# Weight loads held by a copied column, more conversion in the first order, inversion pieces behind softplus, and L in a spare tile

## The chip, the cores and the metric

The kernel runs on one core of one Trainium2 chip. The metric is device time in microseconds (us) of one launch; what is reported for a kernel is the median of several runs. The engines are PE (TensorE, matmuls; PEld is its weight load), DVE (VectorE), ACT (ScalarE), POOL (GpSimd) and SP, whose queue issues the DMA transfers.

## The reference

Two parts follow one another. The first is a delta-rule recurrence over 768 tokens for 4 × 8 heads of width 48; the second is a small MLP with a softplus over the 3072 tokens. The MLP's weights come as 64-bit floats, all other inputs as float32.

```python
def _attn_ref(q, k, v, beta):
    k_n = k / (np.linalg.norm(k, axis=-1, keepdims=True) + 1e-06)
    for t in range(S):
        y[:, :, t] = np.einsum('bhd,bhde->bhe', q[:, :, t], state)
        v_old = np.einsum('bhde,bhd->bhe', state, kt)
        state = state + bt[:, :, :, None] * np.einsum('bhd,bhe->bhde', kt, vt - v_old)

def _moe_ref(x, w_in, w_out):
    h = x @ w_in
    g = np.maximum(h, 0.0) + np.log1p(np.exp(-np.abs(h)))
    return (g @ w_out).astype(np.float32)
```

## The kernel before, in words

**Attention.** The 768 tokens are 12 steps `s` of 64 tokens for all 32 heads. Within a step the recurrence needs the inverse of a triangular matrix per head, built from products of the keys (`gram`, L120 to L149). Two steps (a pair `u`) share one inversion on DVE (`invert`, L186 to L227): a transpose L199, masks L203 and L205, a copy L216 and then a substitution in many small pieces, each a product L220 and a sum L226. `finish` (L229) transposes the result into the tile `tt` (L232, L233). For the first pair only, u = 0 and u = 1 below N16 = 2, the inversion runs in blocks of 16 and `join` (L236) puts the blocks together with two products on PE (L243, L250), using a block L (`LDS`, L211 to L214) that was saved before. Then `cross_a` (L255), `arrange` (L268), `cross_b` (L276), `k_state`, `p_half` with `mask_p`, `u_all` (L312), `y_all` (L332) and `state` (L321) are products on PE, each with a copy on ACT or DVE that the next product waits for. So a step is a chain of short handoffs. The steps 0 and 1 use the blocks of u = 0, the steps 2 and 3 those of u = 1, and so on.

**MLP.** The output of a step, `x`, is a chunk of 256 tokens. For each chunk eight groups of two blocks `f` run: the first product (L462, into `ph`), softplus (ACT L466 to L468, then DVE L470, L472, L473, or L476 alone in the first chunk), and the second product (L445, into `po`), one group later. The first chunk uses float32 weights; later ones use weights split into two parts of a faster type (`split`, L410: ACT L413 and L415, DVE L416), and 18 matmuls for the first product where the first chunk has 6 per group.

**Weights.** The 16 weight tiles come as 64-bit floats and are converted to float32 on the chip (`weights`, L370): for each f ACT takes a magnitude (L381), DVE does four steps (L393, L396, L400, L403) and ACT copies the result (L406). At the start of the conversion of f the load of tile f + 4 is issued (L390 to L392), after a `memset` of one of its columns. It is a generator: each `next` gives one step of four, and `fill(n)` in the first part asks for n steps.

**What sets the order.** The first part, up to the line `fill(5)`, stands under a manual schedule for PE, DVE, ACT and POOL: these engines run it in the order in which it is written. SP and all that follows are ordered by a scheduler that estimates times, within the order of dependences. The main loop interleaves the MLP groups with attention steps; `invert_some(2)` after a group asks for two inversion pieces, and `attend` for as many attention steps as are due. Each engine runs its own list strictly in order, so an instruction that waits holds those behind it. Tiles with the same name share buffers: "gh" and "gl" have two buffers each and hold softplus' result; x0, x1, x2, x4 and w0 to w15 have one.

Of the kernel before, what the change touches and what calls it, by code (L numbers as in the profile page):

```python
# [35 lines left out]
def deltanet_moe(ctx, tc, kT, qT, kN, kI, vN, beta, wts, out):  # L36
# [149 lines left out]
    def invert(u, cT, ncT):  # L186

        n = QB if u < N16 else HB  # L190
        blocks = range(0, HB, n)
        lq = one.tile([P, HB, HB], F32, name="ltq")
        for a in blocks:
            nc.gpsimd.affine_select(
                out=Z[:, a:a + n, a:a + n],
                in_=ncT[:, a:a + n].unsqueeze(1).to_broadcast([P, n, n]),
                compare_op=ALU.is_gt, fill=0.0, base=0, pattern=[[1, n], [-1, n]],
                channel_multiplier=0)
        nc.vector.transpose(lq.rearrange("p j i -> p i j"), LTD[u].rearrange("p q i -> p i q"))  # L199
        yield  # L200
        for a in blocks:
            d = (slice(None), slice(a, a + n), slice(a, a + n))
            nc.vector.tensor_tensor(lq[d], lq[d], Z[d], op=ALU.mult)  # L203
            yield
            nc.vector.tensor_tensor(Z[d], lq[d],  # L205
                                    cT[:, a:a + n].unsqueeze(2).to_broadcast([P, n, n]),
                                    op=ALU.mult)
            yield
        if u < N16:
            for j in range(2):  # L210
                ld = LDS[2 * u + j] = two.tile([P, NP, HB], F32, name="gh")  # L211
                nc.gpsimd.memset(ld[:, :, QB:], 0.0)
                nc.scalar.activation(ld[:, :, 0:QB], LTD[u][:, j * NP:(j + 1) * NP, 0:QB],  # L213
                                     AF.Copy, scale=half)  # L214
        tmp = one.tile([P, HB, HB], F32, name="x0" if u == 0 else "work")
        nc.vector.tensor_copy(Z.rearrange("p a b -> p (a b)")[:, 0:HB * HB:HB + 1], cT)  # L216
        for j in range(n - 2, 0, -1):
            r = n - 1 - j
            for a in blocks:
                nc.vector.tensor_tensor(  # L220
                    tmp[:, a:a + r, 0:j],
                    Z[:, a + j + 1:a + n, a + j:a + j + 1].to_broadcast([P, r, j]),
                    lq[:, a + j:a + j + 1, a:a + j].to_broadcast([P, r, j]), op=ALU.mult)
            for a in blocks:
                z = Z[:, a + j + 1:a + n, a:a + j]
                nc.vector.tensor_tensor(z, z, tmp[:, a:a + r, 0:j], op=ALU.add)  # L226
            yield  # L227
# [8 lines left out]
    def join(s):  # L236

        tt = TT[s // 2][:, s % 2 * NP:(s % 2 + 1) * NP, :]
        w1 = two.tile([P, NP, QB], F32, name="gl")
        pw = ps_a.tile([P, NP, QB], F32, name="pa")  # L240
        for p in range(NP):
            for r in lo + hi:
                nc.tensor.matmul(pw[r, p, :], LDS[s][r, p, :], tt[r, p, QB:HB],  # L243
                                 start=True, stop=True)
        nc.scalar.copy(w1, pw)
        yield
        pz = ps_a.tile([P, NP, QB], F32, name="pa")
        for p in range(NP):
            for r in lo + hi:
                nc.tensor.matmul(pz[r, p, :], tt[r, p, HB:], w1[r, p, :], start=True, stop=True)  # L250
        nc.vector.tensor_tensor(tt[:, :, QB:HB], tt[:, :, QB:HB], pz, op=ALU.subtract)
        nc.vector.transpose(tt[:, :, HB:], tt[:, :, 0:HB])
        yield

    def cross_a(s):  # L255

        tt = TT[s // 2][:, s % 2 * NP:(s % 2 + 1) * NP, :]
        pm = ps_a.tile([P, NP, HB], F32, name="pa")
        for i, e, p, ab, t in quads:
            nc.tensor.matmul(pm[lo[t], p, :], OFF[s][hi[t], p, :], tt[hi[t], p, 0:HB],  # L260
                             start=True, stop=True)
        nc.scalar.activation(OFF[s][lo[0]], pm[lo[0]], AF.Copy, scale=-1.0)
        if s < 2:
            nc.vector.tensor_scalar(OFF[s][lo[1]], pm[lo[1]], -1.0, None, op0=ALU.mult)
        else:
            nc.scalar.activation(OFF[s][lo[1]], pm[lo[1]], AF.Copy, scale=-1.0)
# [9 lines left out]
    def cross_b(s):  # L276

        tt = TT[s // 2][:, s % 2 * NP:(s % 2 + 1) * NP, :]
        pm = ps_a.tile([P, NP, HB], F32, name="pa")
        for i, e, p, ab, t in quads:  # L280
            nc.tensor.matmul(pm[lo[t], p, :], tt[lo[t], p, HB:], OFF[s][lo[t], p, :],  # L281
                             start=True, stop=True)
        for h in range(2):
            copies[s < 2 and h](tt[lo[h], :, HB:], pm[lo[h]])


    def k_state(s):
# [24 lines left out]
    def u_all(s):  # L312
        pus = [ps_a.tile([P, NP // 2, D], F32, name="pa") for e in range(2)]
        for i, e, p, ab, t in quads:
            nc.tensor.matmul(pus[e][tk[ab], i, :], TT[s // 2][tk[t], s % 2 * NP + p, :],  # L315
                             NV[s][tk[t], p, :], start=True, stop=True)
        for e in range(2):
            for ab in range(2):
                copies[s < 2 and ab](be[tk[ab], ab, e, :, C:], pus[e][tk[ab]])  # L319

    def state(s):  # L321
        for g in range(2):
            pd = ps_a.tile([P, 8, D], F32, name="pa")
            for i in range(8):
                for ab in range(2):
                    at = (ab * NP + 8 * g + i) * QW
                    nc.tensor.matmul(pd[dr[ab], i, :], ki[:, ab, 8 * g + i, :],  # L327
                                     big[:, at + C:at + QW], start=True, stop=True)
            for ab in range(2):
                copies[s < 1 and ab](bv[dr[ab], ab, 8 * g:8 * g + 8, C:], pd[dr[ab]])  # L330

    def y_all(s):  # L332

# [36 lines left out]
    def weights():  # L370
# [15 lines left out]
        for f in range(NF):  # L386
            hw, lw = words(f)
            if f + AHEAD < NF:

                ST[f + AHEAD] = one.tile([P, 4 * DM], I32, name=f"w{f + AHEAD}")  # L390
                nc.vector.memset(ST[f + AHEAD][:, 0:1], 0)
                load_weights(f + AHEAD)  # L392
            nc.vector.tensor_scalar(ex.bitcast(F32), ex.bitcast(F32), 2.0 ** -15, 122880.0,  # L393
                                    op0=ALU.max, op1=ALU.min)
            yield
            nc.vector.tensor_scalar(ex, ex, 3, 0x3FFFFFF8, op0=ALU.logical_shift_left,  # L396
                                    op1=ALU.bitwise_and)
            after = magnitude(f + 1) if f + 1 < NF else None
            yield
            nc.vector.scalar_tensor_tensor(ex, hw, -2 ** 30, ex, op0=ALU.bitwise_and,  # L400
                                           op1=ALU.bitwise_or)
            yield
            nc.vector.scalar_tensor_tensor(ex, lw, 29, ex, op0=ALU.logical_shift_right,  # L403
                                           op1=ALU.bitwise_or)
            HF[f] = one.tile([P, 2 * DM], F32, name=f"w{f}")
            nc.scalar.copy(HF[f], ex.bitcast(F32))  # L406
            done[0], ex = f + 1, after
            yield
# [10 lines left out]
    def moe():  # L419
# [4 lines left out]
        for s in range(NS):  # L424
# [26 lines left out]
            for f0 in range(0, NF, 2):  # L451
# [17 lines left out]
                if s:  # L469
                    nc.vector.scalar_tensor_tensor(a, ph, 0.0, a, op0=ALU.max, op1=ALU.add)  # L470
                    g = [two.tile([P, 2, n], F32R, name=name) for name in ("gh", "gl")]
                    nc.vector.tensor_copy(g[0], a)  # L472
                    nc.vector.tensor_tensor(g[1], a, g[0], op=ALU.subtract)  # L473
                else:
                    g = [two.tile([P, 2, n], F32, name="gh")]
                    nc.vector.scalar_tensor_tensor(g[0], ph, 0.0, a, op0=ALU.max, op1=ALU.add)  # L476
                yield
                if late is not None:
                    late()
# [14 lines left out]
    def fill(n):  # L494
        for _ in range(n):
            next(conversion, None)
# [59 lines left out]
            yield  # L556
            background.append(invert(u, *cols[u]))

    background = []

    def invert_some(n):
        for _ in range(n):
            if background and next(background[0], 0) == 0:
                background.pop()

    kas = [one.tile([P, 2, NP, D], F32, name=name) for name in ("tt", "x2")]
    kas = [[t[:, j] for j in range(2)] for t in kas]
    with tc.manual_schedule(engines={ET.PE, ET.DVE, ET.Activation, ET.Pool}):
# [59 lines left out]
        next(jn)  # L628
        for g in range(2):
            mask_p(g, pts[g])  # L630
        run(jn)
        scale_v(0)
        cross_a(0)
        arrange(0)
        fill(2)
        cross_b(0)
        fill(2)
        u_all(0)
        next(nm)
        fill(2)  # L640
        y_all(0)
        jn = join(1)
        next(jn)
        fill(2)
        state(0)
        load_ki(1)
        run(jn)
        cross_a(1)
        arrange(1)
        for _ in range(3):  # L650
            next(nm)
        fill(3)
# [1 line left out]
        cross_b(1)  # L654
        load_v(2)
        cols[1] = run(nm)
        fill(5)

    def attention():
        nonlocal steps_done  # L660
# [110 lines left out]
```

## Time and profile before

| what | value |
|---|---|
| three runs | 718.11, 718.76, 719.0 us (median 718.76) |
| the profiled execution | 716.53 us, span 714.8 us, mean granted TensorE clock 0.956 |
| busy in that span | PE 631.6 us (88%), DVE 457.5 (64%), ACT 369.4 (52%), POOL 30.1 (4%) |
| bytes over DMA | 44.80 MB in 35095 packets |
| weight loads | 16 tiles of 768 KB |

The trace is of one execution. In a row of the timeline or of the chain the first number is the start in us from the span's start, the second the duration in us; "x18" is a number of instructions merged into the row, and in brackets stands how long the engine had been idle before it and what ended that. "issue" is a wait for nothing that the profile shows. Rows of the waits read: engine, tile and line that waited, what it waited for, the sum in us, how often, the longest. In a row of windows, after the stretch and its length, come busy time and instruction count of PE, PEld, DVE, ACT and POOL, then the clock, the DMA share and GB/s.

### The profile page before, as it was taken

To read this page: it belongs to the slowest core of one execution; us is meant where nothing else is said; L and a number is where in the kernel's file an instruction comes from. 1 tells how busy PE (TensorE), PEld (TensorE's weight loads), DVE (VectorE), ACT (ScalarE), POOL (GpSimd) and SP (SyncE) were. 2 spreads that over 40 slices of the span, in tenths; PEclk is the share of its full clock that TensorE was granted. 3 is DMA by queue.
4 is the path that set the end of the run, shared out by engine and by line. 5 is a ranking of instruction groups with operands and counts; after the bars stand their busy time and mean duration, and the time that the engine had idled before them with its cause. 6 is when DMAs were issued, how large, how long until landed. Compare 5 with 4: busy or idle time off the path is not lost.

```text
span 714.8 us, 24068 instructions
## 1 busy us (share of the span) xinstructions
PE 631.6 (88%) x10736; PEld 583.5 (82%) x10736; DVE 457.5 (64%) x976; ACT 369.4 (52%) x681; POOL 30.1 (4%) x56
## 2 busy tenths in 40 slices
PE   4448877858998899998899997999998999999997
PEld 3447655537898898997899997899997999999997
DVE  5834799866746993466993467984449964454443
ACT  3222377819844356464357465365663556544443
POOL 3100100000000000000001000001000000000000
PEclk9999899979797999998999999899999999999999
DMA  9974250000022021032031130120310300201000
GB/s 224 367 280 120 68 137 10 0 2 25 4 71 78 23 68 46 13 88 61 23 86 38 48 100 27 45 57 25 73 31 24 79 2 25 59 3 33 1 23 22
DMA packets 35095, 44.80 MB, mean 63 GB/s; under 512 B 21776, under 2 KB 27184, under 8 KB 34992
## 3 DMA queue, kind: packets, MB, share of 16 engines
q1 hardware_dynamic: 34992, 43.27, 21.2%
q8 instruction: 84, 1.38, 0.8%
q14 instruction: 19, 0.16, 0.1%
HBM read 36.27 MB, written 4.72 MB: 57 GB/s over the span
## 4 chain that ended last, share of the span: by engine, by line
PE 65%; DVE 21%; issue 6%; ACT 6%; DMA 2%; SPq 0%; POOL 0%; DVEq 0%; ACTq 0%; POOLq 0%
PE po L445 24%; PE ph L462 23%; DVE work L220 3%; PE pa L342 3%; DVE Z L226 3%; PE pa L301 2%; PE pa L260 2%; PE pa L327 2%; PE pa L281 2%; DVE ltq L199 1%; DVE a L470 1%; DVE big L308 1%; DVE ex L403 1%; PE pa L315 1%; PE pa L131 1%
## 5 line engine op out<-in xcount | busy, mean ns | idle before, releaser
L462 PE MATMUL ph<-x,w 128*128 128x256 f32 x1680 | 247.4, 299 | 16.6 <-DVE a L470 9.0
L462 PEld LDWEIGHTS ph<-x,w 128*128 128x128 f32 x1680 | 228.3, 197 | 26.0 <-DVE a L470 9.7
L445 PE MATMUL po<-w,gh 128*128 128x384 f32 x768 | 214.9, 367 | 8.1 <-DVE gh L472 4.2
L466 ACT ACTIVATE a<-ph 128x512 f32<-128x512 f32 x96 | 57.4, 598 | 214.3 <-PE ph L462 203.4
L470 DVE SCALAR_TENSOR_TENSOR a<-ph,a 128x512 f32<-128x512 f32 x88 | 60.6, 689 | 155.5 <-ACT a L468 155.1
L445 PEld LDWEIGHTS po<-w,gh 128*128 128x128 f32 x768 | 139.3, 195 | 20.3 <-issue 6.6
L445 PE MATMUL po<-w,gl 128*128 128x384 f32 x352 | 121.2, 344 | 0.2 <-DVE gl L473 0.2
L445 PEld LDWEIGHTS po<-w,gl 128*128 128x128 f32 x352 | 67.8, 193 | 1.1 <-DVE gl L473 0.7
L473 DVE TENSOR_TENSOR gl<-a,gh 128x512 fp32r<-128x512 f32 x88 | 60.7, 690 | 3.8 <-PE po L445 0.7
L467 ACT ACTIVATE a<-a 128x512 f32<-128x512 f32 x96 | 60.7, 633 | 2.8
L468 ACT ACTIVATE a<-a 128x512 f32<-128x512 f32 x96 | 60.7, 632 | 2.4
L220 DVE TENSOR_TENSOR work<-Z,ltq 128x84 f32<-128x84 f32 (+14 forms) x148 | 44.0, 304 | 3.3 <-ACT gh L213 0.6
L226 DVE TENSOR_TENSOR Z<-Z,work 128x84 f32<-128x84 f32 (+14 forms) x148 | 44.1, 305 | 2.9
L472 DVE CAST gh<-a 128x512 fp32r<-128x512 f32 x88 | 38.0, 432 | 7.8 <-PE po L445 4.4
L342 PEld LDWEIGHTS pa<-big 128*64 128x64 f32 x768 | 26.0, 145 | 7.6 <-ACT big L319 2.6
L342 PE MATMUL pa<-big 128*64 128x64 f32 x768 | 28.8, 232 | 3.4 <-ACT big L319 2.1
L308 DVE TENSOR_TENSOR big<-pa,maskP 64x512 f32<-64x512 f32 x44 | 30.2, 686 | 1.6 <-PE pa L301 1.0
L301 PE MATMUL pa<-big,kt 48*64 48x64 f32 x704 | 27.7, 231 | 1.6 <-ACT off L118 0.9
L274 POOL MEMSET tt<- 32x512 f32 x24 | 13.2, 550 | 368.1 <-PE pa L260 203.2
L319 ACT COPY big<-pa 64x384 f32<-64x384 f32 x44 | 20.6, 472 | 13.1 <-PE pa L315 12.5
L301 PEld LDWEIGHTS pa<-big,kt 48*64 48x64 f32 x704 | 25.1, 145 | 2.0 <-ACT off L118 1.1
L330 ACT COPY big<-pa 48x384 f32<-48x384 f32 x42 | 19.9, 474 | 8.9 <-PE pa L327 8.3
(104 smaller groups left out, 648.4 us busy)
## 6 DMA issues: line engine op xcount, KB each, us to landing
w<-wts SPq DMA_DIRECT2D x16, 768.0 KB, 11.7
kt<-kT SPq DMA_DIRECT2D x24, 192.0 KB, 4.2
big<-qT SPq DMA_DIRECT2D x24, 192.0 KB, 4.1
nv<-vN SPq DMA_DIRECT2D x12, 384.0 KB, 4.1
ki<-kI SPq DMA_DIRECT2D x24, 192.0 KB, 3.5
out<-ex SPq DMA_DIRECT2D x24, 192.0 KB, 1.9
ka<-kN SPq DMA_DIRECT2D x8, 384.0 KB, 3.2
x<-x SPq DMA_DIRECT2D x66, 32.0 KB, 2.1
```

The source lines that it names most:

```text
L220: nc.vector.tensor_tensor(tmp[:, a:a + r, 0:j], Z[:, a + j + 1:a + n, a + j:a + j + 1].to_broadcast([P, r, j]), lq[:, a + j:a + j + 1, a:a ...
L226: nc.vector.tensor_tensor(z, z, tmp[:, a:a + r, 0:j], op=ALU.add)
L301: nc.tensor.matmul(pt[tk[ab], i, :], kts[s % 3][dr[ab], 8 * g + i, :], bv[dr[ab], ab, 8 * g + i, 0:C], start=True, stop=True)
L342: nc.tensor.matmul(py[tk[ab], i, :], big[:, at + C:at + 2 * C], big[:, at:at + C], start=True, stop=True)
L445: nc.tensor.matmul(po[:, h, 0:DM], g[b][:, f - f0, h * P:(h + 1) * P], weight(f, a, DM, DM), start=(f == 0 and i == 0), stop=end)
L462: nc.tensor.matmul(ph[:, f - f0], weight(f, a, k * P, P), xr[b][k], start=(c == 0), stop=(c == len(terms1) * NK - 1))
L466: nc.scalar.activation(a, ph, AF.Abs)
L467: nc.scalar.activation(a, a, AF.Exp, scale=-1.0)
L468: nc.scalar.activation(a, a, AF.Ln, bias=1.0)
L470: nc.vector.scalar_tensor_tensor(a, ph, 0.0, a, op0=ALU.max, op1=ALU.add)
L472: nc.vector.tensor_copy(g[0], a)
L473: nc.vector.tensor_tensor(g[1], a, g[0], op=ALU.subtract)
```

## The change

Four edits are made together.

1. L, the lower block for the join, no longer takes a "gh" buffer of softplus; it lies in a tile of the name x1 (u = 0) or x2 (u = 1), which is free at that time. The join's intermediate `w1`, before in a "gl" buffer, lies in the same tile.
2. The column of the weight tile f + 4 that was set by a `memset`, which depends on nothing, is now copied from `ex`, the magnitude of conversion f. So the load of tile f + 4 waits for that magnitude.
3. For step 1 the second copies of `cross_a`, `cross_b` and `u_all`, which were on DVE, go to ACT; those of `state(0)` as well.
4. In the first part the calls of `fill` ask for 25 steps of conversion instead of 16, and some stand earlier; in the loop the inversion pieces are issued after the last softplus instruction that was written down before them.

```diff
         if u < N16:
+            spare = one.tile([P, 2, NP, HB + QB], F32, name=f"x{u + 1}")
             for j in range(2):
-                ld = LDS[2 * u + j] = two.tile([P, NP, HB], F32, name="gh")
+                ld = LDS[2 * u + j] = spare[:, j, :, 0:HB]
+                LDS[2 * u + j, 1] = spare[:, j, :, HB:]
...
-        w1 = two.tile([P, NP, QB], F32, name="gl")
+        w1 = LDS[s, 1]
...
-        if s < 2:
+        if s < 1:
             nc.vector.tensor_scalar(OFF[s][lo[1]], pm[lo[1]], -1.0, None, op0=ALU.mult)
...
-            copies[s < 2 and h](tt[lo[h], :, HB:], pm[lo[h]])
+            copies[s < 1 and h](tt[lo[h], :, HB:], pm[lo[h]])
...
-                copies[s < 2 and ab](be[tk[ab], ab, e, :, C:], pus[e][tk[ab]])
+                copies[s < 1 and ab](be[tk[ab], ab, e, :, C:], pus[e][tk[ab]])
...
-                copies[s < 1 and ab](bv[dr[ab], ab, 8 * g:8 * g + 8, C:], pd[dr[ab]])
+                nc.scalar.copy(bv[dr[ab], ab, 8 * g:8 * g + 8, C:], pd[dr[ab]])
...
-                nc.vector.memset(ST[f + AHEAD][:, 0:1], 0)
+                nc.vector.tensor_copy(ST[f + AHEAD][:, 0:1], ex[:, 0:1])
...
-                    nc.vector.tensor_tensor(g[1], a, g[0], op=ALU.subtract)
+                    softplus[0] = nc.vector.tensor_tensor(g[1], a, g[0], op=ALU.subtract)
...
     def invert_some(n):
-        for _ in range(n):
-            if background and next(background[0], 0) == 0:
-                background.pop()
+        with tc.issue_after(softplus[0].ins):
+            for _ in range(n):
+                if background and next(background[0], 0) == 0:
+                    background.pop()
...
+        fill(2)
         run(jn)
         scale_v(0)
+        fill(2)
         cross_a(0)
         arrange(0)
         fill(2)
         cross_b(0)
-        fill(2)
+        fill(3)
         u_all(0)
         next(nm)
-        fill(2)
+        fill(4)
         y_all(0)
         jn = join(1)
         next(jn)
-        fill(2)
+        fill(4)
         state(0)
...
         arrange(1)
+        fill(2)
...
-        fill(5)
+        fill(3)
```

The lines of the changed kernel are three higher from L211 on (L243 becomes L246, L260 becomes L263, L445 becomes L448, and so on), up to the softplus of the later chunks; numbers behind a tile's name are those of its buffers.

First, the queue of SP in the first part, behind the load of w3. Before, it holds the tiles w8 to w15 next:

```order
L368 DMA w3_114<-wts 128x1536
L368 DMA w8_1413<-wts 128x1536
L368 DMA w9_1424<-wts 128x1536
L368 DMA w10_1525<-wts 128x1536
L368 DMA w11_1536<-wts 128x1536
L368 DMA w12_1564<-wts 128x1536
L368 DMA w13_1575<-wts 128x1536
L368 DMA w14_1610<-wts 128x1536
L368 DMA w15_1621<-wts 128x1536
L95 DMA ka_1844<-kN 128x768
L79 DMA kt0_74<-kT 48x1024 x2
L368 DMA w4_740<-wts 128x1536
```

After the change, in the same place:

```order
L371 DMA w3_114<-wts 128x1536
L95 DMA ka_1840<-kN 128x768
L79 DMA kt0_74<-kT 48x1024 x2
L371 DMA w4_631<-wts 128x1536
L371 DMA w5_749<-wts 128x1536
L371 DMA w6_795<-wts 128x1536
L91 DMA nv_1178<-vN 128x768
L371 DMA w7_845<-wts 128x1536
L83 DMA big_77<-qT 48x16x64 x2
L363 DMA x0_849<-x4_850 16x256 x6
L371 DMA w8_970<-wts 128x1536
```

The keys of later steps and w4 to w7 have moved ahead of w8, and w9 to w15 follow further down, each behind its own hold.

Second, PE's list at the second use of the join's first product (L243, of the step pair u = 1, step 2). Before it stands between the first products of the first chunk's last groups and the second products of the same chunk:

```order
L462 MATMUL ph<-x_832,w_1725 128x256 x3
L462 MATMUL ph<-x_832,w_1731 128x256 x3
L243 MATMUL pa<-tt,gh 32x16 x64
L445 MATMUL po<-w_1676,gh 128x384 x2
L445 MATMUL po<-w_1684,gh 128x384 x2
L462 MATMUL ph<-x_1303,w_1769 128x256 x9
L462 MATMUL ph<-x_1303,w_1774 128x256 x9
L445 MATMUL po<-w_1725,gh 128x384
L445 MATMUL po<-w_1731,gh 128x384
```

After the change (now L246) it stands among the groups of the second chunk, whose x is x_1326:

```order
L448 MATMUL po<-w_1770,gh 128x384 x2
L448 MATMUL po<-w_1770,gl 128x384
L465 MATMUL ph<-x_1326,w_2087 128x256 x7
L246 MATMUL pa<-tt,x_1643 32x16 x64
L465 MATMUL ph<-x_1326,w_2199 128x256 x9
L465 MATMUL ph<-x_1326,w_2204 128x256 x2
L448 MATMUL po<-w_1775,gh 128x384 x2
```

All second products of the first chunk, three first products and one second product of the second chunk have moved ahead of the join.

Third, DVE's list in an inversion of the later pairs (u = 3; Z and ltq are its tiles, a, gh and gl those of softplus). Before, some way into it, where the first softplus step stands:

```order
L220 TENSOR_TENSOR work_4546<-Z_79,ltq_4524 128x7x24
L226 TENSOR_TENSOR Z_79<-Z_79,work_4546 128x7x24
L220 TENSOR_TENSOR work_4546<-Z_79,ltq_4524 128x8x23
L226 TENSOR_TENSOR Z_79<-Z_79,work_4546 128x8x23
L220 TENSOR_TENSOR work_4546<-Z_79,ltq_4524 128x9x22
L226 TENSOR_TENSOR Z_79<-Z_79,work_4546 128x9x22
L220 TENSOR_TENSOR work_4546<-Z_79,ltq_4524 128x10x21
L226 TENSOR_TENSOR Z_79<-Z_79,work_4546 128x10x21
L470 SCALAR_TENSOR_TENSOR a_4515<-ph_4496,a_4515 128x512
L220 TENSOR_TENSOR work_4546<-Z_79,ltq_4524 128x11x20
L472 CAST gh_4520<-a_4515 128x512
L226 TENSOR_TENSOR Z_79<-Z_79,work_4546 128x11x20
```

After the change, from the inversion's start on:

```order
L199 STREAM_TRANSPOSE ltq_4518<-work_4268 128x32x32
L203 TENSOR_TENSOR ltq_4518<-ltq_4518,Z_79 128x1024
L473 SCALAR_TENSOR_TENSOR a_4563<-ph_4544,a_4563 128x512
L205 TENSOR_TENSOR Z_79<-ltq_4518,cT_4357 128x1024
L475 CAST gh_4568<-a_4563 128x512
L219 COPY Z_79<-cT_4357 128x32
L223 TENSOR_TENSOR work_4540<-Z_79,ltq_4518 128x30
L476 TENSOR_TENSOR gl_4569<-a_4563,gh_4568 128x512
L229 TENSOR_TENSOR Z_79<-Z_79,work_4540 128x30
L473 SCALAR_TENSOR_TENSOR a_4611<-ph_4592,a_4611 128x512
L223 TENSOR_TENSOR work_4540<-Z_79,ltq_4518 128x2x29
L475 CAST gh_4616<-a_4611 128x512
```

The softplus steps, of which ten pairs of inversion pieces stood ahead before, now begin behind the first mask.

More of the change, by code (lines that the diff above doesn't have):

```diff
@@ L472, in moe @@
                     nc.vector.tensor_copy(g[0], a)
-                    nc.vector.tensor_tensor(g[1], a, g[0], op=ALU.subtract)
+                    softplus[0] = nc.vector.tensor_tensor(g[1], a, g[0], op=ALU.subtract)
                 else:
                     g = [two.tile([P, 2, n], F32, name="gh")]
-                    nc.vector.scalar_tensor_tensor(g[0], ph, 0.0, a, op0=ALU.max, op1=ALU.add)
+                    softplus[0] = nc.vector.scalar_tensor_tensor(g[0], ph, 0.0, a, op0=ALU.max,
+                                                                 op1=ALU.add)
                 yield
@@ L557, in chunk @@
             background.append(invert(u, *cols[u]))
-    background = []
+    background, softplus = [], [None]
     def invert_some(n):
-        for _ in range(n):
-            if background and next(background[0], 0) == 0:
-                background.pop()
+        with tc.issue_after(softplus[0].ins):
+            for _ in range(n):
+                if background and next(background[0], 0) == 0:
+                    background.pop()
     kas = [one.tile([P, 2, NP, D], F32, name=name) for name in ("tt", "x2")]
```

## The prediction

> **What bounds the kernel now.** I read the page first, then the chain that ended last, then windows, then the waits of PE and DVE.
>
> ```profile
> PE 631.6 (88%) x10736; PEld 583.5 (82%) x10736; DVE 457.5 (64%) x976; ACT 369.4 (52%) x681; POOL 30.1 (4%) x56
> 68.89:150.76 81.87, 59.24 (x720) 42.37 (x720) 72.56 (x162) 52.16 (x84) 3.55 (x6) 0.91 0.17 49
> 170.00:200.00 30.00, 26.62 (x759) 25.21 (x758) 20.11 (x29) 23.58 (x38) 2.25 (x4) 0.83 0.02 4
> ```
>
> The first row is the whole span of 714.8 us: PE is idle for 714.8 − 631.6 = 83.2 us, and that is all that a reordering can win, apart from time lost to a lowered clock. The window rows give busy time of PE, PEld, DVE, ACT, POOL, then granted clock, DMA share and GB/s. From 68.89 to 150.76 DVE is busy for 72.56 of 81.87 us and PE for 59.24: conversion and the second inversion set the pace. Ahead of that lies a chain of short steps:
>
> ```profile
> 18.00 13.21 SPq L368 DMA_DIRECT2D w<-wts  x10
> q8 instruction: 84, 1.38, 0.8%
> 30.76 3.44 issue
> 36.23 0.61 PE pa L250 x28
> 36.84 3.43 issue
> 40.27 1.60 PE pa L250 x100
> 42.37 0.96 PE pa L260 x28
> 43.32 3.14 issue
> 46.47 1.20 PE pa L260 x36
> 47.68 0.60 ACT off L262
> 48.30 0.70 DVE off L264
> 49.04 1.94 PE pa L281 x60
> 51.01 0.58 ACT tt L284
> 54.38 0.83 ACT w L406
> 67.40 0.71 issue
> ```
>
> Within L250's 128 matmuls PE stops after 28, and within L260 again after 28: 100 + 28 = 128 matmuls with their 128 weight loads apart. [...] These stops last 3.44, 3.43 and 3.14 us while ten weight tiles, issued within 13.21 us from 18.00, are still landing. With little DMA under way they are shorter:
>
> ```profile
> 178.13 0.73 PE L243 MATMUL pa<-tt,gh 32*32 32x16 f32 x40 [2.04 <-issue]
> 193.44 0.45 PE L291 MATMUL pa<-big,kt 48*64 48x48 f32 x17 [1.25 <-issue]
> ```
>
> **The change, part by part.** The four DVE steps of a conversion, grouped (count, then busy time and mean ns) between 68.8 and 151 us:
>
> ```profile
> L400 DVE SCALAR_TENSOR_TENSOR ex<-w,ex 128x768 int32<-128x768 int32 x14 | 13.2, 954 | 0.1
> L403 DVE SCALAR_TENSOR_TENSOR ex<-w,ex 128x768 int32<-128x768 int32 x14 | 13.2, 956 | 0.0
> L393 DVE TENSOR_SCALAR ex<-ex 128x768 f32<-128x768 f32 x14 | 8.0, 580 | 0.0
> L396 DVE TENSOR_SCALAR ex<-ex 128x768 int32<-128x768 int32 x14 | 7.9, 586 | 0.1
> ```
>
> Together 0.954 + 0.956 + 0.580 + 0.586 = 3.08 us.
>
> *Weight hold.* The eight early loads leave SP's queue (first pair of orders above) and w4 waits for the first conversion. Nothing is lost by it as long as a tile lands before its turn: four conversions of 3.08 us on DVE lie between hold and use. The three stops cost 10.0 us; at the mean of the two quiet ones, 1.65, they cost 5.0, a gain of 5.0. Bounds: 0 if the load is not their cause, 10.0 − 3 × 0.71 = 7.9 by the shortest row. [...]
>
> [...]
>
> *More conversion in the first order.* One conversion's last two DVE steps and its ACT copy, 0.95 + 0.96 + 0.83 = 2.74 us, now stand ahead of ACT L262 (L265 of the changed kernel). PE's L260 covers them with 0.96 + 1.20 us and its own stop. I take 1.1 us as the cost for this and the other inserted steps; bounds 0 and 2.74. The DVE is otherwise idle there. So the wide stage starts at 68.89 − 5.0 + 1.1 = 65.0 instead of 68.89, where L250 of join 1 ends.
>
> *Spare L tile, and the order of the second join.* This is the largest term.
>
> ```profile
> 119.62 0.22 DVE L216 COPY Z<-cT 128x32 f32<-128x32 f32 x1
> 139.22 0.32 POOL L212 MEMSET gh<- 128x256 f32 x1 [10.29 <-PE po L445]
> 139.45 0.51 ACT L213 ACTIVATE gh<-work,half 128x256 f32<-128x256 f32 x1
> 139.99 0.26 DVE L220 TENSOR_TENSOR work<-Z,ltq 128x14 f32<-128x14 f32 x2 [0.56 <-ACT gh L213]
> 148.86 1.90 DVE L232 STREAM_TRANSPOSE tt<-Z 128x1024 f32<-128x1024 f32 x1
> 150.91 1.90 PE L243 MATMUL pa<-tt,gh 32*32 32x16 f32 x128 [9.15 <-DVE tt L232]
> 111.48 2.85 PE L445 MATMUL po<-w,gh 128*128 128x384 f32 x8 [0.87 <-DVE gh L476]
> 153.68 4.65 PE L445 MATMUL po<-w,gh 128*128 128x384 f32 x8 [0.87 <-DVE gh L476]
> 170.25 1.26 PE L250 MATMUL pa<-gl,tt 32*32 32x16 f32 x128
> ```
>
> The inversion was ready to go on at 119.84, but L lay in a softplus buffer, so POOL, ACT and then DVE waited until 139.99. PE, whose order has the second join ahead of the last output products, stood for 9.15 us and then ran eight matmuls in 4.65 instead of 2.85 us. After the change all first-chunk products, three second-chunk groups and one output group stand ahead of that join (second pair of orders). In before PE had done all of that at 170.25, or 168.35 without the 1.90 of L243 itself.
>
> When is tt there after the change? From the same start to L235 the order holds two conversions fewer on DVE. Two conversions are 2 × 3.08 = 6.2 us. The step-1 copies that go to ACT take some 2.5 us with them (the two cross copies at the 0.70 of L264, the rest smaller); against it two more splits (0.95 each, as L400, whose shape they have), two more first-chunk softplus steps and one of the second chunk come ahead, together about 5 us at some 0.7 a step. Net −3.6 of 72.56 busy, so 69. Idle time was 81.87 − 72.56 = 9.3; I keep it and add 2.7, since inversion pieces now stand behind softplus steps that wait for ACT. That is 81 us, tt at 65.0 + 81 = 146, and the join at 148 with 2 us for its place in PE's order. Gain at this point, all above included: 168.35 − 148 = **20.3 us**. Bounds: join at 141 (most of the idle time gone) and at 157 (idle time doubled).
>
> *Copies of step 1 on ACT, and the stage behind the join.* From 170 to 200 ACT is busy for 23.58 of 30 us. After the change ten splits (2 × 0.83 each, by the ACT copy above, 16.6 us) and the softplus and copies of the second chunk stand on ACT behind the join, by my estimate as much as the PE work that is left of that chunk, and the chunk-2 attention steps come in one cluster. I take **4 us** lost; bounds 2 and 7.
>
> *Inversion pieces behind softplus, pairs 2 to 5.*
>
> ```profile
> PE ph L462 <- DVE a L470: 9.0, 4, 4.6
> PE po L445 <- DVE gh L472: 4.2, 2, 2.8
> 439.86 0.63 ACT L468 ACTIVATE a<-a 128x512 f32<-128x512 f32 x1
> 447.37 0.69 DVE L470 SCALAR_TENSOR_TENSOR a<-ph,a 128x512 f32<-128x512 f32 x1
> 448.11 4.21 PE L462 MATMUL ph<-x,w 128*128 128x256 f32 x18 [4.64 <-DVE a L470]
> 345.33 3.78 PE L462 MATMUL ph<-x,w 128*128 128x256 f32 x18 [2.17 <-DVE a L470]
> 459.44 2.30 PE L462 MATMUL ph<-x,w 128*128 128x256 f32 x18
> ```
>
> Softplus was ready on ACT at 440.49 and its DVE step ran at 447.37, behind some twenty inversion pieces; PE stood for 4.64 us. All such waits are 9.0 + 4.2 = 13.2 us. After them PE is slow: the same 18 matmuls take 4.21 and 3.78 against 2.30, so 1.91 and 1.48 more; at a mean of 1.7 for the three longest that is 5.1, in all 18.3 us. I take 15 of it. [...] Against the 15: the tie stretches an inversion over nine or ten groups instead of seven (third pair of orders), and attention steps then follow one another on PE without output products between in chunks 8 and 10. From L262 at 47.68 to L281 at 49.04 PE had 1.36 us of handoff with no cover, and the two copies after L281 (0.58 and about 0.7) cost as much: 2.7 us per cluster, 6 us for two with their slow clock. Net gain **9 us**; bounds 16 (one cluster, all waits gone) and 0.
>
> *Sum.* 20.3 − 4 + 9 = 25.3 us. The profiled execution took 716.53 us, so 691.2; the median of the runs, 718.76, lies 2.2 above it: **693 us**.
>
> **Rivals.** *The slower one: the inversion comes late.* A held inversion that isn't done when the next pair's cross product L260 needs tt stops PE, as the join did at 150.91: 9.15 us and 4.65 − 2.85 = 1.80 us after it, 10.95 in each of pairs 2 to 5, 43.8 us. Against gains of 20.3 − 4 + 15 = 31.3 that gives 12.5 us slower, 731 us. It decides from 31.3 / 4 = 7.8 us per pair. For it: two fewer DVE pieces run per group, and the tie has no due time. Against it: DVE is busy for only 64% of the span, and the stretched inversions still end within their pair in the new order. Chance 0.09.
>
> *The first order delays itself.* If the nine added conversion steps, about 0.77 us each on DVE (3.08 / 4), all fall on the chain, they cost 6.9 instead of 1.1, and if the steady part gains nothing, 20.3 − 5.8 − 4 = 10.5 us is left: 708 us. For it: DVE and ACT run strictly in their written order. Against it: the stops in which they would be hidden are in the chain above. Chance 0.15.
>
> *The stops are not from the loads*, so that the weight hold does nothing: 5.0 us less, 698 us. [...] Against it: 1.25 and 2.04 with the DMA quiet. Chance 0.12.
>
> **How the numbers follow.** The forecast has 0.60. All favourable bounds together give 27.4 − 2 + 16 = 41 us (677 us), all unfavourable ones 11.4 − 7 + 0 = 4 us (714 us); the range is 677 to 711, which leaves out the slower rival and part of the worst sums. About 0.2%, 1.4 us, is what a measurement of this kernel can tell from no change. Faster: 0.60 + 0.15 + 0.12 = 0.87; slower 0.09; within 0.2%: 0.04, for sums that cancel.
>
> **What would show it.** Right: the stops at 30 to 47 us fall below 2.1 us; POOL and ACT no longer wait for L445 before the inversion; PE's L246 of the second join starts near 148 with little idle time before it; the DVE-for-softplus waits in PE's list fall from 13.2 us to under 3. Wrong: stops of 3 us with the DMA quiet; L265 waiting for ACT's conversion copies by more than 3 us; L246 after 157; or waits of PE's L263 for tt in pairs 2 to 5 of 8 us and more.

## The result, and the profile after

The changed kernel takes 675.33 us (four runs, 670.16 to 678.78) against 718.43 us (715.87 to 719.0): a ratio of 0.9401, 95% interval 0.9325 to 0.9476. The prediction was 693 with a range down to 677, so it had the direction and missed the size: about 43 us were won where 25 were forecast. The profiled execution took 672.51 us, 44.0 less than the profiled one of before. In two of the experiments below (e7, e9) a single execution took over 1100 us; it is left out.

The page of the changed kernel, busy time by engine:

```profile
PE 612.4 (91%) x10736; PEld 571.7 (85%) x10736; DVE 451.9 (67%) x970; ACT 372.5 (56%) x687; POOL 30.5 (5%) x56
```

PE's idle time fell from 83.2 to 670.8 − 612.4 = 58.4 us, and PE's busy time itself fell by 631.6 − 612.4 = 19.2 us for the same 10736 matmuls: 19.2 of the 44.0 us are work that runs at a higher clock (0.971 on the mean against 0.956) or closer together.

To see where, both spans are cut at the same instructions: the end of join 1 (where the wide stage starts), then the last output copies of chunk 0, of chunk 1 and of chunk 9. Windows of the kernel before (stretch and length, busy time of PE, PEld, DVE, ACT, POOL, then clock, DMA share, GB/s):

```profile
0.00:68.89 68.89, 35.82 (x1409) 32.43 (x1409) 37.41 (x112) 21.77 (x44) 10.63 (x26) 1.00 0.82 255
68.89:166.11 97.22, 73.08 (x903) 52.65 (x903) 77.45 (x167) 57.69 (x94) 3.55 (x6) 0.89 0.15 43
166.11:238.08 71.97, 66.60 (x1578) 63.02 (x1578) 46.02 (x86) 48.51 (x92) 3.51 (x5) 0.86 0.16 44
238.08:647.06 408.98, 392.23 (x6419) 372.44 (x6411) 269.63 (x568) 212.73 (x408) 12.40 (x19) 0.97 0.18 46
647.06:714.80 67.74, 63.87 (x443) 63.00 (x441) 26.98 (x45) 28.68 (x49) 0.00 (x0) 0.99 0.05 18
```

The same stretches of the changed kernel:

```profile
0.00:64.90 64.90, 33.13 (x1409) 29.84 (x1409) 43.10 (x114) 25.80 (x50) 10.81 (x26) 0.97 0.71 197
64.90:145.24 80.34, 69.38 (x776) 52.43 (x775) 64.81 (x151) 56.49 (x93) 3.94 (x6) 0.87 0.37 111
145.24:213.90 68.66, 61.79 (x1700) 57.83 (x1700) 43.01 (x77) 49.06 (x91) 3.52 (x5) 0.98 0.17 46
213.90:603.01 389.11, 384.26 (x6419) 368.58 (x6414) 273.99 (x585) 212.37 (x408) 12.26 (x19) 0.99 0.18 48
603.01:670.80 67.79, 63.87 (x443) 63.00 (x441) 27.00 (x45) 28.73 (x49) 0.00 (x0) 0.99 0.05 18
```

The stages give 4.0, 16.9, 3.3, 19.9 and −0.05 us, 44.0 in all. In the last stage PE is busy for 63.87 us in both, and it did not move. The first two were forecast (3.9, and 20.3 with it at the join); the fourth is twice what was forecast, and the third has the other sign. The second cut, the last output copy of chunk 0, does not divide the work alike: the 128 matmuls of the join's first product stand ahead of it in the kernel before (903 matmuls in the second stage, 1578 in the third) and behind it in the changed one (776 and 1700). At the forecast's own cut, the join, 19.0 us are won and 5.2 behind it (from 168.35 to 238.08 before, 149.38 to 213.90 after).

The chain of the changed kernel at its start, and the join of step 2 in the timeline:

```profile
30.10 2.73 issue
35.48 1.25 issue
42.29 0.83 ACT w L409
43.13 0.50 ACT off L265
60.45 3.73 issue
```

```profile
40.73 1.17 PE L263 MATMUL pa<-tt,off 32*32 32x32 f32 x36 [0.96 <-issue]
149.38 1.26 PE L246 MATMUL pa<-tt,x 32*32 32x16 f32 x128
```

The three stops that cost 10.0 us are now 2.73, 1.25 and 0.96 us (the third in front of L263, no longer on the chain), 4.94 in all; 5.0 was forecast. The stop in the second product of join 1, 0.71 before, is 3.73 here; in e1 and e12 it is 1.80 and 1.53. A weight tile is issued just ahead of it, at 61.64 us, but what sets its length was not tested. ACT's conversion copy stands right ahead of L265, as the order said. The join starts at 149.38 (forecast 148) with no idle time in its row, where PE stood for 9.15 us before. What is left of PE's waits for softplus of the later chunks, of 13.2 us before:

```profile
PE ph L465 <- DVE a L473: 0.9, 1, 0.9
PE po L448 <- DVE gh L475: 0.7, 1, 0.7
```

### The profile page after: what moved, and what is told of

Its sections match the earlier page's. It is cut to its first block, busy times and chain, and to the rows that moved or that the text cites. A ratio compares the mean times of both kernels' runs of the same rounds, so it can differ in the third digit from the quotient of the medians.

```text
span 670.8 us, 24090 instructions
## 1 busy us (share of the span) xinstructions
PE 612.4 (91%) x10736; PEld 571.7 (85%) x10736; DVE 451.9 (67%) x970; ACT 372.5 (56%) x687; POOL 30.5 (5%) x56
## 4 chain that ended last, share of the span: by engine, by line
PE 77%; ACT 8%; DVE 7%; issue 5%; DMA 2%; POOL 1%; SPq 0%; ACTq 0%; DVEq 0%; POOLq 0%
PE ph L465 29%; PE po L448 27%; PE pa L345 4%; PE pa L304 3%; PE pa L330 2%; PE pa L318 2%; PE pa L284 2%; PE pa L131 2%; PE pa L294 2%; DMA big<-qT 1%; ACT tt L275 1%; PE pa L263 1%; PE pa L127 1%; DVE ex L406 1%; DVE ex L403 1%
## 5 line engine op out<-in xcount | busy, mean ns | idle before, releaser
L465 PE MATMUL ph<-x,w 128*128 128x256 f32 x1680 | 240.9, 294 | 2.2 <-DVE a L473 0.9
L465 PEld LDWEIGHTS ph<-x,w 128*128 128x128 f32 x1680 | 224.6, 192 | 10.1 <-DVE w L419 1.2
L448 PE MATMUL po<-w,gh 128*128 128x384 f32 x768 | 208.0, 357 | 3.7 <-DVE gh L479 2.4
L448 PEld LDWEIGHTS po<-w,gh 128*128 128x128 f32 x768 | 135.0, 190 | 13.6 <-DVE gh L479 3.2
L473 DVE SCALAR_TENSOR_TENSOR a<-ph,a 128x512 f32<-128x512 f32 x88 | 60.5, 689 | 106.6 <-ACT a L471 106.2
L448 PE MATMUL po<-w,gl 128*128 128x384 f32 x352 | 119.2, 339 | 0.0
L448 PEld LDWEIGHTS po<-w,gl 128*128 128x128 f32 x352 | 66.3, 188 | 0.5 <-DVE gl L476 0.2
L475 DVE CAST gh<-a 128x512 fp32r<-128x512 f32 x88 | 37.7, 428 | 7.7 <-PE po L448 5.6
L345 PEld LDWEIGHTS pa<-big 128*64 128x64 f32 x768 | 27.8, 150 | 10.9 <-ACT big L322 7.1
L345 PE MATMUL pa<-big 128*64 128x64 f32 x768 | 31.0, 238 | 6.7 <-ACT big L322 5.7
L322 ACT COPY big<-pa 64x384 f32<-64x384 f32 x46 | 21.7, 473 | 19.5 <-PE pa L318 18.7
L277 POOL MEMSET tt<- 32x512 f32 x24 | 13.1, 545 | 402.3 <-PE pa L263 224.9
```

The source lines that it names most:

```text
L345: nc.tensor.matmul(py[tk[ab], i, :], big[:, at + C:at + 2 * C], big[:, at:at + C], start=True, stop=True)
L448: nc.tensor.matmul(po[:, h, 0:DM], g[b][:, f - f0, h * P:(h + 1) * P], weight(f, a, DM, DM), start=(f == 0 and i == 0), stop=end)
L465: nc.tensor.matmul(ph[:, f - f0], weight(f, a, k * P, P), xr[b][k], start=(c == 0), stop=(c == len(terms1) * NK - 1))
```

## The experiments

Each ratio is to runs of the kernel before on the same chip. Stretches are between the same points as above; "steady" is from the end of chunk 1 to the end of chunk 9.

**The changed kernel again.** No edit.

> The changed kernel once more, unaltered, on the chip on which the next three run. Both theories: 670 to 679 us, as its four runs so far (670.16 to 678.78); ratio to before 0.933 to 0.948.

> The changed kernel once more, unaltered, as the measure for e10 and e11 on the same chip: 670 to 681 us, with run times that fall as the mean granted clock rises (668.4 us of span at 0.974, 677.1 at 0.956 so far).

Measured 678.04 us (0.9434, 0.9379 to 0.949) and 676.29 us (0.9421, 0.9382 to 0.9461). All fourteen executions of the changed kernel lie between 669.14 and 680.77 us with a median of 677.2, the lower edge of the forecast's range; the two fastest had clocks of 0.982 and 0.974, the slowest 0.952. All three profiled executions (672.51, 671.9 and 674.62 us) lie below that median. The steady stretches of these two profiles are 387.4 and 391.1 us, chunk 1 takes 71.35 and 70.79 us. So the 68.66 us of chunk 1 in the first profile was a lucky one, and differences under some 4 us of single executions say little here. The steady stretch of e12 has the clock of the kernel before, 0.97, and next to none of its idle time (391.13 − 387.32 = 3.8 us):

```profile
213.99:605.12 391.13, 387.32 (x6419) 371.92 (x6414) 273.86 (x585) 211.92 (x407) 12.25 (x19) 0.97 0.18 48
```

**The tie taken away**, all else as changed:

```diff
 def invert_some(n):
-    with tc.issue_after(softplus[0].ins):
-        for _ in range(n):
+    for _ in range(n):
...
```

> The changed kernel with the inversion pieces no longer behind softplus; weight hold, fills, spare L tile and copies as changed. Theory T1 (the tie brings what was gained from the end of chunk 0 on, some 23 of 43 us: waits of PE for softplus and the slow clock behind them): the waits of PE for L473 and L475 come back at some 13 us in all, and the time is 675 + 18 to 23 = 693 to 698 us. Rival T2 (the steady gain comes from the other start, which shifts what the scheduler puts side by side, not from the tie): waits under 6 us, 675 to 683 us.

693.03 us, ratio 0.965 (0.961 to 0.9689); 15.0 us above e1. The waits come back, and the steady stretch is as long as before the change:

```profile
PE ph L465 <- DVE a L473: 10.2, 5, 4.3
PE po L448 <- DVE gh L475: 2.9, 3, 2.0
```

```profile
216.47:623.62 407.15, 390.67 (x6421) 371.21 (x6414) 270.16 (x569) 212.27 (x408) 12.62 (x19) 0.97 0.17 46
```

13.1 us of waits, but 407.15 − 389.11 = 18.0 us of time. T1 holds, at its lower edge: by the medians the tie is worth 15.0 us, less than the profiled executions show.

**The tie alone**, on the kernel before, from the third pair on (with L in a softplus buffer it can't stand at the second inversion: L would hold the buffer that the softplus in front of it needs; `pieces()` is the loop that stood there):

```diff
 def invert_some(n):
...
+    if steps_done >= 3:
+        with tc.issue_after(softplus[0].ins):
+            pieces()
+    else:
+        pieces()
```

> The kernel before with the tie alone, from the third pair on. Theory T1 (the tie by itself brings the whole steady gain, by taking PE's waits for softplus and the slow clock after them away): stretch from the end of chunk 1 to the end of chunk 9 falls from 409 to some 388 to 390 us, the time to 696 to 701 us. Rival T2 (the tie needs the other parts): stretch above 398 us, time 706 us or more.

Ratio 0.9784 (0.9757 to 0.9811), about 701.5 us; the time is at the upper edge of what T1 gave. The profile of it:

```profile
239.51:632.15 392.64, 386.87 (x6419) 371.00 (x6415) 273.80 (x585) 212.11 (x407) 12.26 (x19) 0.98 0.18 48
```

```profile
PE pa L243 <- DVE tt L232: 9.7, 1, 9.7
```

The steady stretch is 16.3 us shorter by the tie alone, a little above the 388 to 390 forecast, and the wait at the join is untouched. The tie does its work without the other parts.

**The tie from the third pair on only**, all else as changed.

> The changed kernel with the tie only from the third pair on (inversions of pairs 2 to 5); the second inversion, which ends at the join of step 2, is untied. Theory T1 (the tie pays only where an inversion stood ahead of softplus, in pairs 2 to 5): the steady stretch from the end of chunk 1 to the end of chunk 9 stays near 388 us (untied 407), waits of PE for L473 and L475 under 3 us, time 676 to 681 us. Rival T2 (the tied second inversion, with the join moved behind it, matters as much): 684 us or more.

673.6 us, 0.9413 (0.9364 to 0.9462), as the changed kernel, a little below T1's 676 to 681; steady 388.78, and no wait of PE for L473 or L475 is left. The tied second inversion brings nothing that these runs can tell.

**As e5, with L back in gh and gl.**

> As e5, and L back in the gh and gl buffers of softplus (the tie has to be left out for the second inversion there, since L would hold the buffer that the softplus in front of it needs). Theory T1 (the spare tile and the place of the join that goes with it are worth what PE stood and ran slow there): POOL and ACT wait for L448 again, PE stands some 8 to 10 us at the join of step 2 and the time is 10 to 16 us above e5. Rival T2 (with two conversions fewer behind the first order DVE is free earlier, and the wait for the buffer lies beside conversion): within 4 us of e5.

691.73 us, 0.9651 (0.9625 to 0.9677): 18.1 above e5, more than T1's 10 to 16, with the chain of waits of the kernel before back:

```profile
POOL gh L213 <- PE po L446: 38.6, 2, 33.7
PE pa L244 <- DVE tt L233: 8.5, 1, 8.5
PE po L446 <- DVE gh L477: 6.5, 2, 5.6
```

**The spare L tile alone**, on the kernel before.

```diff
-                ld = LDS[2 * u + j] = two.tile([P, NP, HB], F32, name="gh")
+                ld = LDS[2 * u + j] = spare[:, j, :, 0:HB]
```

> The kernel before with the spare L tile alone. Theory T1: the second inversion no longer waits for L213, PE no longer stands 9.15 us at the join; the part alone brings 10 to 16 us, 702 to 708 us. Rival T2 (DVE was busy with conversion in 116 to 137 us anyway, so that the inversion ends hardly earlier and the part needs the other fills): under 5 us, 714 us or more.

703.36 us, 0.9811 (0.9782 to 0.9841): 13.6 us by the ratio (0.0189 × 717), 12.7 by the medians, T1. The join now starts at 150.35 without a wait, though in a place of PE's order by my count of its rows some eight us of work further on; the waits for softplus remain:

```profile
PE ph L464 <- DVE a L472: 10.0, 4, 4.2
PE po L447 <- DVE gh L474: 4.3, 2, 2.2
```

**The memset back**, all else as changed.

```diff
-                nc.vector.tensor_copy(ST[f + AHEAD][:, 0:1], ex[:, 0:1])
+                nc.vector.memset(ST[f + AHEAD][:, 0:1], 0)
```

> The changed kernel with the memset back in place of the copied column, so that w11 to w15 are loaded early again. [...]

682.83 us, 0.9511 (0.9475 to 0.9546), 4.8 above e1. The chain of waits at its start:

```profile
30.31 3.16 issue
...
36.12 3.72 issue
...
42.88 2.88 issue
```

All three stops are back, 9.76 us against 4.94 in the changed kernel, and the time rose by about as much, near the 5.0 us that the prediction gave the hold. That they come with the loads is shown: the four profiles in which the loads are issued early (before, e3, e8, e9) have 9.75 to 10.0 us in these three stops, the other ten 4.0 to 6.4.

**The fills of before**, all else as changed.

> The changed kernel with the fills of before (16 steps of conversion in the first part instead of 25). Theory T1 (stage up to the join is bound by DVE, two more conversions of 3.08 us in it): the join's first product of step 2 starts 5 to 6 us later and the time is 679 to 682 us. Rival T2 (the added fills delay the first chain as much as they relieve the stage): within 2 us of the changed kernel, 673 to 677 us.

681.8 us, 0.9503 (0.9464 to 0.9542), 3.8 above e1; the join of step 2 starts at 152.04 against 147.79 in e1. The time is T1's, the join comes 4.25 us later instead of 5 to 6. The fills do cost something on the first chain (join 1 ends at 63.04 us here, at 65.33 in e1 and 64.74 in e12) and win more than that behind it.

**The copies of step 1 and of state(0) as before**, all else as changed.

```diff
-        if s < 1:
+        if s < 2:
```

(and the three other copy choices likewise)

> The changed kernel with the copies of step 1 and of state(0) shared between ACT and DVE as before. Theory T1 (they load ACT, which is nearly full behind the join, by more than they relieve DVE ahead of it, the forecast's term of 4 us): 2 to 4 us faster than the changed kernel, 672 to 676 by the median. Rival T2 (the stage up to the join is bound by DVE and takes the 2.5 us that it gets back): join 2 to 3 us later, 678 to 681 us.

Ratio 0.9519 (0.9467 to 0.9571), about 684 us: 6 to 7 us slower than the changed kernel, above the range of either theory. The interval is 3.8 us to each side. The join comes at 152.50 instead of 147.3 to 149.4, so it takes back 3 to 5 us of DVE time, T2; and later one long wait of PE stands on ACT, which stands on a load of keys:

```profile
203.88 0.84 ACT L158 ACTIVATE ka<-ka 128x768 f32<-128x768 f32 x1 [5.85 <-DMA ka<-kN]
```

```profile
PE pa L127 <- ACT big L333: 7.2, 3, 6.0
```

T1, by which these copies are behind the forecast's 4 us lost, falls: with the copies on ACT the kernel is faster, not slower. Whether this load came late because of the copies or only because the scheduler placed it otherwise is open.

**Three pieces per group**, and the same with the tie from the third pair on only.

```diff
-            invert_some(2)
+            invert_some(3)
```

> The changed kernel with three inversion pieces asked for per group instead of two, so that the first steps of chunk 8 have output products between them again while chunk 10 keeps its cluster. Theory T1 (a cluster of attention steps costs what the prediction charged, about 3 us, most of it a half-speed stretch of PE's clock): the half-speed stretch near 460 us goes, the pair of chunks 6 and 7 falls from 98.4 to some 95 us, time 2 to 4 us below the changed kernel. Rival T2 (three pieces ahead of a softplus step bring PE's waits back): waits for L473 and L475 over 4 us, time 2 us or more above it. Rival T3 (the clusters cost nothing): within 1 us.

> The tie from the third pair on only (as e5) with three pieces per group. If e5 and three pieces are each worth what T1 says: 2 to 4 us below the changed kernel, 671 to 675 us by the median. T3: as the changed kernel.

e10 took 675.95 us (0.9432, 0.9406 to 0.9457), as the changed kernel on that chip; e11 took 670.67 (0.9352, 0.9325 to 0.9379), 5.6 us below it and the fastest of all. Windows of the changed kernel for the pairs of chunks 4 and 5, 6 and 7, 8 and 9:

```profile
312.35:407.52 95.17, 94.79 (x1639) 90.40 (x1637) 69.32 (x149) 54.07 (x106) 3.35 (x5) 1.00 0.20 56
407.52:505.91 98.39, 97.70 (x1646) 93.57 (x1649) 68.40 (x148) 53.55 (x104) 3.34 (x5) 0.97 0.17 46
505.91:603.01 97.10, 96.08 (x1523) 93.42 (x1515) 67.34 (x142) 50.81 (x97) 2.08 (x4) 0.98 0.14 35
```

The same three pairs of e10:

```profile
324.17:418.96 94.79, 94.41 (x1626) 90.70 (x1625) 69.06 (x149) 54.44 (x105) 3.56 (x5) 1.00 0.20 57
418.96:513.05 94.09, 94.09 (x1652) 90.02 (x1652) 67.30 (x148) 53.48 (x104) 3.34 (x5) 1.00 0.18 48
513.05:608.13 95.08, 94.37 (x1523) 91.48 (x1516) 66.65 (x142) 50.65 (x96) 2.08 (x4) 1.00 0.14 36
```

The two pairs with a cluster lose 4.3 and 2.0 us against e10, and their clock of 0.97 and 0.98 goes back to 1.00; the pair without one is the same. In e1 the two pairs lose 2.8 and 2.1 us, in e12 4.2 and 2.1. So a cluster does cost 2 to 4 us, as T1 says, though the whole time is the one that T3 gave. In e10 the gain is given back earlier: chunk 1 ends at 221.47 us instead of 213.99 in e12. There the second inversion, tied and three pieces at a time, stands differently; e11, which leaves it untied, ends chunk 1 at 217.22 and keeps most of the gain. That it is the tie there and not the whole order around it was not taken apart further.

## Why the prediction was right in direction and wrong in size

**Stops and first chain: right, in part by luck.** Forecast 3.9 us (5.0 won, 1.1 paid), measured 4.0, and e3 brings the stops back with the early loads: 9.76 us there and 10.0 in the kernel before, where the DMA share from 30 to 50 us is 0.85, against 4.94 in the changed kernel, where it is 0.31. The rival by which they are not from the loads falls. By what way a load lengthens a stop no trace shows: the rows say only "issue". The sum is nearer than its parts: the fills cost 1.7 to 2.3 us by e4 where 1.1 was taken, and the stop in the second product of join 1 grew by 3.0 us in this profile, which is no term of the sum.

**Spare tile and join: right.** Forecast 20.3 us at the join, measured 168.35 − 149.38 = 19.0; e1 and e12, whose joins start at 147.79 and 147.34, give 20.6 and 21.0. DVE is busy for 68.6 us from the end of join 1 until the first half of tt is there, and the forecast had 69. It is idle for 15.6 us in that time (13.7 in e1 and e12) where 12 was taken, while the 2 us for the join's place in PE's order were not needed; the two errors cancel in part. One by one the parts are worth 13.6 for the spare tile (e8), 4.8 for the hold (e3), 3.8 for the fills (e4) and 3 to 5 for the copies (e7), more than the 19.0 together: they overlap. The rival of a first order that delays itself falls with e4.

**Stage behind the join: wrong sign.** The step that failed is "I take **4 us** lost", for the splits, softplus and copies that "stand on ACT behind the join". From the join to the end of chunk 1, 5.2 us are won in the first profile, 2.5 in e1 and 3.1 in e12. Chunk 1 took 68.66 to 71.35 us in these three against 71.97. ACT is busy for 49.06 of 68.66 us there, against 48.51 of 71.97 before: it had the room, and PE's idle time in that stage is 6.9, 5.5 and 4.9 us against 5.4. The copies that were charged here win 6 to 7 us by e7; the splits and the cluster of chunk 2 were not taken apart. The charge was wrong by 6 to 9 us. The higher figure is in part luck with the clock: of chunk 1, 10.2 us went to a lowered clock before, 1.7 in the first profile of the changed kernel, 6.8 in e1 and e12.

**Inversion behind softplus: right mechanism, mis-sized.** The step that failed is "Net gain **9 us**", 15 won and 6 paid. By the medians the tie is worth 15.0 us (e2) and by the ratio 15.5 (e9); the steady stretch is 19.9 us shorter in the first pair of profiles, 17.8 to 21.6 over three. The 6 us for two clusters was about right: 4.3 + 2.0 = 6.3 by e10. So the gross gain is 21 to 22 us by whole runs, 24 to 28 by these profiles, where the rows gave 18.3 and "I take 15 of it" cut that further, for which no row spoke.

Windows of 0.5 us over the steady stretch divide the 19.9 into three parts. Idle time of PE: 16.8 us before, 4.9 after, so 11.9 won, nearly all of it the 13.2 − 1.6 us of waits for softplus. Time lost to a lowered clock: 10.2 us before, of which 6.8 lie behind the three long waits (the prediction had 5.1) and 3.4 behind a stop of 1.81 us that ends at 329.33 us, marked "issue"; 5.1 after, all of it at the two clusters. The other 2.8 us are busy time of PE beyond what the clock took, which the prediction didn't count and these runs don't explain.

Only the first part surely comes from the tie. Idle time is 16.5 to 17.4 us in the three profiles without it (before, e2, e8) and 2.9 to 5.8 in the eleven with it. The loss to the clock is 10.2, 10.2 and 5.1 us without it, and 5.1, 5.1 and 10.2 in three profiles of the changed kernel: it changes from one execution to the next. The slow stretch behind that stop, for one, stands in e5 and e12 too and not in the first profile and e1, so 3.4 of the 19.9 us are luck.

**Sum.** At the forecast's own cuts the terms are 19.0 instead of 20.3, 5.2 instead of −4, and 19.9 instead of 9: −1.3 + 9.2 + 10.9 = 18.8, which but for 0.05 us at the end is the 44.0 − 25.3 = 18.7 by which the profiled execution missed. By the medians it is 693 − 675.33 = 17.7. Both errors were charges or discounts against the gain. The slower rival, an inversion that comes late, falls: PE's L263 waits for tt only once, for 0.5 us on the first chain, and what attention costs in the steady stretch is the cluster at 2 to 4 us.

The parts, each measured by itself, add up: 13.6 (spare, e8) + 15.5 (tie, e9: 0.0216 × 717) + 4.8 (hold, e3) + 3.8 (fills, e4) + 6.5 (copies, e7: 0.9519 less the mean 0.9428 of e1 and e12, times 717, the kernel before in us) = 44 us against 41 to 43 for the whole. That they agree so well is in part chance: each has an interval of 2 to 4 us to each side, two were added to the kernel before and three taken out of the changed one, and the spare tile is worth 18.1 us when it is taken out instead (e6 against e5).

## What to carry to other kernels

When one engine carries both a long background job and short steps that the bound engine waits for, put the job's pieces behind each short step: here that took the waits from 13.2 us to 1.6. Count them in full and don't discount what the rows add up to without a row that speaks for it; take the slow clock behind such waits from several profiles, since it changed between executions (5.1, 5.1 and 10.2 us of the steady stretch in three profiles of one kernel). A buffer borrowed from a rotating pool for a long-lived value cost 13.6 us by e8 and 18.1 by e6; look for a tile that is free at that time. And time a part against several executions where one kernel scatters as this one did, from 669.14 to 680.77 us.

## What the runs showed of the hardware that was not expected

The scatter of the changed kernel (669 to 681 us) goes with the granted clock: over its fourteen executions the correlation of time and clock is −0.83. In windows of 3 us between 75 and 640 us, the slow stretches of twelve profiles (all but e3 and e4; one that begins earlier aside) lose 1.7, 3.4, 5.1 or 6.8 us each, which is 3.4, 6.8, 10.2 or 13.7 us at a clock of 0.50, the lowest that any window of 0.5 us shows in the first two profiles. Windows of 3 us in the changed kernel around the cluster of chunk 8:

```profile
456.00:459.00 3.00, 2.31 (x131) 2.19 (x130) 1.50 (x3) 2.92 (x6) 1.53 (x3) 1.00 0.02 5
459.00:462.00 3.00, 3.00 (x114) 2.88 (x116) 0.05 (x1) 2.59 (x5) 0.54 (x2) 0.82 0.02 5
462.00:465.00 3.00, 3.00 (x60) 2.79 (x54) 1.79 (x4) 0.15 (x1) 0.00 (x0) 0.50 0.00 0
465.00:468.00 3.00, 3.00 (x88) 2.65 (x88) 1.72 (x3) 0.64 (x2) 0.00 (x0) 0.55 0.03 5
468.00:471.00 3.00, 3.00 (x90) 2.89 (x87) 1.38 (x2) 2.41 (x5) 0.00 (x0) 1.00 0.73 194
```

PE had been idle for only 0.69 us, in the first window, and then ran at half clock for about 6.8 us while it was busy all the time: 3 × (0.18 + 0.50 + 0.45) = 3.4 us lost, five times the wait itself. That the wait is the cause is not shown. The slow stretch at the cluster of chunk 10 (559.5 to 563.5 us) follows a wait of 0.26 us; in both clusters the 128 matmuls of L263, on 32x32 tiles, stand just ahead, and in e10, where output products stand between the attention steps of chunk 8 and behind the L263 of chunk 10, neither stretch is slow. So waits of 0.69 and 0.26 us were followed by a slow stretch, and one of 1.69 us that ends at 300.69 us in the same profile was not. The same place is slow in one execution and not in another: chunk 1 took 68.66, 71.35 and 70.79 us in three profiles, of which 1.7, 6.8 and 6.8 us went to a lowered clock. What decides it was not tested.
